# A new order for the first batch, the first scores of each batch and the last batch's weight splits in a packed-attention and SwiGLU kernel

## Chip, cores and metric

The kernel runs on one core of a Trainium2 chip. The metric is the device time of one execution in microseconds. "Before" is the median of three runs: 1436.34 us (1432.2 to 1437.11).

## What is computed

The reference has three parts, joined by one activation matrix x of 4608 tokens by 512:

```python
# attention: 8 batches, 8 heads, 576 positions, head size 64, 32 packing rows
p_packed = sm_attn(p, k, v)                 # "pack": softmax(p k^T / 8) v
out      = sm_attn(q, p_packed, p_packed)   # "unpack"
x = out.transpose(0, 2, 1, 3).reshape(4608, 512)
# SwiGLU
xn = x / sqrt(mean(x * x) + 1e-6) * rms_g
x  = (silu(xn @ w_gate) * (xn @ w_val)) @ w_out      # 512 -> 1536 -> 512
# bilinear
a, b = x @ w1, x @ w2
return ((a * b) @ w3) @ w_out2
```

The weights arrive as 64-bit floats. The kernel reads them as pairs of 32-bit words and builds 32-bit floats on the chip ("conversion").

## The kernel before

The program is one hand-written order. Python generators emit instructions, each engine runs its own instructions in the order of emission, and all loads and stores are issued by SyncE (SP), also in order. A wait at the head of an engine's queue holds all that stands behind it there.

**Conversion.** A `[128, 512]` block of 64-bit weights (0.52 MB) is loaded by `load64` (L99). `convert` then issues two ScalarE activations (`c_h` L108, `c_y` L109), two VectorE instructions (`c_t` L111, and the joining of sign and magnitude L112) and one GpSimd addition (L114). The gate and value weights `wgv` need 24 conversions, four for each of six column groups g.

**Attention of a batch.** `pack(b)` makes the packed rows: scores of p against k (PE L181), maximum (VectorE L185), exponential (ScalarE L188), transposes (PE L197) with copies (L198 on ScalarE, L199 on VectorE), the product with v (PE L208), scaling (L216), a transpose (L220) and the copies `bdP1T` (L224), `gP1T` (L226) and `bdG` (L239). `unpack(b)` takes q: scores against `bdP1T` (PE L262), transposes to `a2` on VectorE (L266), maximum, subtraction, exponential, sum and division, a transpose back to `a2T`, the norm of each token, and at the end the normalised activations split into a high part `ah` and a rest `al` (L55 on ScalarE, L56 on VectorE), as the matmuls need them.

**Dense units.** `wb_unit(b, g)` multiplies `gP1T` of batch b with column group g of `wgv` (PE L337) and splits the product into `wbh` and `wbl`. `dense_units(b)` then has 48 units, eight for each g; a unit is six matmuls into one PSUM bank (L376). Even units are evicted by a tanh on ScalarE (`th` L382) and VectorE (L383), odd ones by ScalarE (`vl` L387) and GpSimd (`ht` L388). Four banks ("gv") rotate through the units, two slots of two banks each ("at") through everything else. `wb_unit(b, g + 1)` stands after the fourth unit of group g.

**What sets the order.** `planned` runs `dense_units(b)` and, after the units whose numbers stand in a table, one step of another generator: `PACK` for `pack(b + 2)`, `UNPACK` for `unpack(b + 1)`, and two conversions of `w_out` per batch. In batch 0 the last 12 conversions of `wgv` take that place. Ahead of the first dense unit, the "front" is ordered by a string of letters: p (a step of pack 0 and then pack 1), u (unpack 0), c (a whole conversion, and the load of the block three further on), w (`wb_unit(0, 0)`), l (loads of later batches). In the last batch `first_loads` takes the place of the attention: its first step issues three loads of `w_out` rows, and each later step splits one row block into `wo_h` and `wo_l` (L55, L56), for the matmuls that follow the dense part. Its steps stand after the units 0, 3, 6, and so on up to 42.

After the dense part come the product with `w_out` (L566) and the bilinear stage (L811), which the change leaves alone.

Of the kernel before, what the change touches and what calls it, by code (L numbers as in the profile page):

```python
# [16 lines left out]
B, H, S, D = 8, 8, 576, 64  # L17
# [3 lines left out]
NC = H // 2  # L21
# [11 lines left out]
def packed_attention_swiglu_bilinear(ctx: ExitStack, tc, qT, kT, v, pT, rms_g, w_gv, w_out,  # L33
                                     w1, w2, w3T, w_out2, out):
    nc = tc.nc
# [49 lines left out]
    def load_k(b, parts=1):  # L85
        load("k", kT, b, 2, parts)

    def load_q(b):
        load("q", qT, b, 2)
# [7 lines left out]
    def load64(src):  # L97
        w = cv_of[0].tile([128, 512, 2], I32, tag="w64", name="w64", bufs=ahead64[0] + 1)
        nc.sync.dma_start(out=w.rearrange("p n t -> p (n t)"), in_=src.bitcast(I32))  # L99
        return w  # L100

    def convert(dst, w, shape):
        cv = cv_of[0]
        h = cv.tile([128, 512], F32, tag="c_h", name="c_h", bufs=2)
        y = cv.tile([128, 512], I32, tag="c_y", name="c_y", bufs=2)
        t = cv.tile([128, 512], I32, tag="c_t", name="c_t")
        d = dst.bitcast(I32)
        nc.scalar.activation(out=h, in_=w[:, :, 1].bitcast(F32), func=AF.Copy, scale=float(2.0 ** -112))  # L108
        nc.scalar.activation(out=y, in_=w[:, :, 0].bitcast(U32), func=AF.Copy, scale=float(2.0 ** -29))  # L109
        hi = h.bitcast(I32)  # L110
        nc.vector.tensor_scalar(out=t, in0=hi, scalar1=3, scalar2=None, op0=ALU.logical_shift_left)  # L111
        nc.vector.scalar_tensor_tensor(out=d, in0=shape(hi), scalar=-2 ** 31, in1=shape(t),  # L112
                                       op0=ALU.bitwise_and, op1=ALU.bitwise_or)
        nc.gpsimd.tensor_tensor(out=d, in0=d, in1=shape(y), op=ALU.add)  # L114

    def converting(jobs, take):


        n64 = ahead64[0]
        ahead = [load64(src) for src, *_ in jobs[:n64]]  # L120
        yield
        for i, job in enumerate(jobs):
            take(ahead.pop(0), *job[1:])
            if i + n64 < len(jobs):
                ahead.append(load64(jobs[i + n64][0]))
            yield
# [9 lines left out]
    converted = set()  # L136
    c_o_bufs = [2]

    def gv_weight(w, g, c):
        convert(wgv[:, c, :, 256 * g:256 * g + 256], w, lambda x: x.rearrange("p (a n) -> p a n", a=2))  # L140
        converted.add((g, c))

    def out_weight(w, dst):
        store_later(4, out=dst, in_=as_f32(w))
# [4 lines left out]
    pTs = att.tile([128, NC, B, NP], F32, name="pTs")  # L149
    nc.sync.dma_start(out=pTs, in_=pT)  # L150
    load_k(0, 2)
    gvw = converting([(w_gv[g, c], g, c) for g in range(6) for c in range(NC)], gv_weight)
# [92 lines left out]
    def unpack(b):  # L245
# [19 lines left out]
        for a, t in enumerate(ts):  # L265
            nc.vector.transpose(out=a2.rearrange("p e t n -> p e (t n)")[:, :, HALF * a:HALF * a + HALF],  # L266
                                in_=t[:, :, :HALF])
        yield
        if b:
            load_q(b + 2)  # L270
        for e in range(2):
            nc.vector.tensor_reduce(out=mx2[:, e], in_=a2[:, e], axis=AX.X, op=ALU.max)
            yield
            nc.vector.tensor_tensor(out=a2[:, e], in0=a2[:, e], in1=wide(mx2[:, e]), op=ALU.subtract)  # L274
            nc.scalar.activation(out=a2[:, e], in_=a2[:, e], func=AF.Exp, scale=SCALE)
            yield
# [52 lines left out]

    def wb_unit(b, g):  # L330
        gP1T = res["gP1T", b]
        while not all((g, c) in converted for c in range(NC)):
            next(gvw)
        t = slot("at")
        for c in range(NC):
            for e in range(2):
                nc.tensor.matmul(t[32 * c:32 * c + 32, e, :], lhsT=gP1T[64 * e:64 * e + 64, c, :],  # L337
                                 rhs=wgv[64 * e:64 * e + 64, c, :, 256 * g:256 * g + 256],
                                 start=True, stop=True, tile_position=(64 * e, 32 * c), skip_group_check=True)
        hi = dp.tile([128, 2, 512], F32R, tag="wbh", name="wbh", bufs=2)  # L340
        lo = dp.tile([128, 2, 512], F32R, tag="wbl", name="wbl", bufs=2)
        for e in range(2):
            split(hi[:, e], lo[:, e], t[:, e], nc.vector)
        wb[b, g] = (hi, lo)
# [58 lines left out]
    def drain(gen):  # L403
        for _ in gen:
            pass
# [16 lines left out]
    def chained(*gens):  # L422
        for g in gens:
            yield from g

    next(gvw)
    load_v(0)
    load_q(0)
    load_k(1)

    def planned(main, *others):

        for n, _ in enumerate(main):
            for at, gen in others:
                for _ in range(at.count(n)):
                    next(gen, None)
        for at, gen in others:
            for n in at:
                assert n < 60
            drain(gen)  # L440

    def wb_first():
        wb_unit(0, 0)
        yield

    def later():
        load_q(1)
        load_k(2)
        yield
        load_q(2)  # L450
        yield

    front = dict(p=chained(pack(0), pack(1)), u=unpack(0), c=gvw, w=wb_first(), l=later())
    for x in "pp c c p c pp c pp u c u u p u p u c w u u u c u uu p u c uu l pp c uu c uu pp c l c c":
        if x != " ":
            next(front[x])
    for x in "puw":
        drain(front[x])  # L460
    ow = converting([(w_out[128 * i:128 * i + 128, :], wo_d[128 * i:128 * i + 128, :]) for i in range(NF)], out_weight)

    PACK = [8, 8, 16, 31, 32, 40, 43]
    UNPACK = [0, 1, 3, 4, 6, 11, 13, 15, 17, 24, 24, 25, 31, 32, 40, 41, 42, 44]
    for b in range(B - 1):
        others = [(UNPACK, unpack(b + 1))]
        if b + 2 < B:
            others.insert(0, (PACK, pack(b + 2)))
        if b == 0:
            others.append(([1, 3, 5, 9, 12, 14, 18, 20, 22, 26, 28, 30], gvw))  # L470
        else:
            others.append(([21, 35], some(ow, 2)))
        planned(dense_units(b), *others)
# [42 lines left out]
    def first_loads():  # L516
        rows = [wo_d[128 * kk:128 * kk + 128, :] for kk in range(NF)]
        ahead = [fetch(x) for x in rows[:3]]
        yield
        for i in range(NF):  # L520
            split(wo_h[:, i], wo_l[:, i], ahead.pop(0), nc.gpsimd if i % 2 else nc.vector)
            if i + 3 < NF:
                ahead.append(fetch(rows[i + 3]))
            else:
                fetch_h(i + 3 - NF)
            yield
        fetch_h(3)
        for n in range(2):
            split_h(n)
            yield  # L530

    planned(dense_units(B - 1), (list(range(0, 45, 3)), first_loads()))
    flush()
    dp_ctx.close()
    wraw_ctx.close()
# [363 lines left out]
```

## Time and profile before

| | |
|---|---|
| median of the runs | 1436.34 us (1432.2 to 1437.11) |
| the profiled execution | 1431.36 us, span 1429.2 us |
| busy share of the span | PE 95%, VectorE (DVE) 55%, ScalarE (ACT) 38%, GpSimd (POOL) 34% |
| mean granted TensorE clock | 0.984 of full speed |
| chain that ended last, by engine | PE 80%, DVE 7%, ACT 3%, DMA 3%, issue 2% |
| first dense unit | 63.9 us after the span's start |
| last batch's dense units | from about 480.7 us |

The page of the profile gives busy time by engine. The timeline gives single instructions with start and duration, and in brackets the idle time of the engine just before one and what ended it. The view of waits sums such idle time by line and by what ended it, for a stretch. The view of windows gives the busy time of each engine in a stretch, with the granted clock.

### The profile page before, as it was taken

What the parts mean: (1) busy time and instruction counts of PE and PEld (TensorE: products, weight loads), DVE (VectorE), ACT (ScalarE), POOL (GpSimd) and SP (SyncE); (2) the same over time, 40 slices, a digit from 0 to 9 for tenths busy, and PEclk for the clock granted to TensorE, in tenths of its full rate; (3) what the DMA queues carried; (4) which work ended last, traced back from release to release, by engine and by line L of the source; (5) the groups of instructions that cost most, each with busy time, mean ns of one, the idle gap of its engine ahead of it and who ended that gap; (6) DMA issues with size and microseconds to landing.
All of it is one profiled execution on the core that took longest, in us unless ns stands there. A gap on an engine that the chain in (4) does not pass through costs nothing.

```text
span 1429.2 us, 22605 instructions
## 1 busy us (share of the span) xinstructions
PE 1353.3 (95%) x8824; PEld 1119.0 (78%) x8824; DVE 787.5 (55%) x1267; ACT 545.7 (38%) x1080; POOL 489.7 (34%) x438
## 2 busy tenths in 40 slices
PE   4579999999999899999999999999999999999988
PEld 2358878788788788888888877887888788788887
DVE  4787566766766547736177855335335343534443
ACT  3455455555555566525155542113112111211211
POOL 2456445445455452203034503322222222222111
PEclk9689999999999999999999999999999999999999
DMA  9853454443221357735369875434442643444263
GB/s 312 290 197 108 160 192 137 148 155 111 107 97 75 134 170 264 238 124 162 122 226 407 325 288 225 164 148 160 165 155 81 243 155 124 171 155 149 82 250 124
DMA packets 65562, 253.65 MB, mean 177 GB/s; under 512 B 7344, under 2 KB 7344, under 8 KB 55344
## 3 DMA queue, kind: packets, MB, share of 16 engines
q1 hardware_dynamic: 65456, 252.21, 49.8%
q8 instruction: 69, 1.13, 0.3%
q14 instruction: 37, 0.30, 0.1%
HBM read 185.08 MB, written 67.11 MB: 176 GB/s over the span
## 4 chain that ended last, share of the span: by engine, by line
PE 80%; DVE 7%; ACT 3%; DMA 3%; issue 2%; POOL 0%; SPq 0%; DVEq 0%; ACTq 0%; POOLq 0%
PE gv L811 24%; PE gv L376 17%; PE at L566 13%; PE gv L784 7%; PE at L784 7%; PE gv L566 5%; PE gv L658 3%; PE at L337 2%; DMA w<-ws_d 2%; DVE th L383 1%; PE at L292 1%; DVE a L274 1%; DVE wbl L56 1%; DVE wgv L112 1%; ACT vl L387 1%
## 5 line engine op out<-in xcount | busy, mean ns | idle before, releaser
L811 PE MATMUL gv<-xh,w 128*128 128x512 f32 (+1 forms) x1120 | 287.3, 371 | 10.1 <-DMA w<-ws_d 6.4
L55 ACT ACTIVATE hh<-hr 128x512 fp32r<-128x512 f32 (+1 forms) x148 | 91.0, 618 | 419.1 <-DVE hr L779 332.0
L811 PEld LDWEIGHTS gv<-xh,w 128*128 128x128 f32 x1120 | 201.1, 190 | 49.4 <-DMA w<-ws_d 7.6
L388 POOL TENSOR_TENSOR ht<-th,vl 128x288 f32<-128x288 f32 x192 | 163.7, 860 | 178.1 <-ACT vl L387 95.8
L376 PE MATMUL gv<-ah,wbh 128*128 128x288 f32 x768 | 178.7, 314 | 16.0 <-ACT vl L387 12.4
L376 PEld LDWEIGHTS gv<-ah,wbh 128*128 128x128 f32 x768 | 122.6, 190 | 67.6 <-issue 26.9
L838 POOL TENSOR_TENSOR u<-u,c 128x512 f32<-128x512 f32 (+1 forms) x40 | 63.9, 1598 | 319.9 <-DVE u L779 319.9
L376 PE MATMUL gv<-al,wbh 128*128 128x288 f32 x768 | 167.1, 298 | 0.0
L779 DVE TENSOR_TENSOR hr<-gv,hr 128x512 f32<-128x512 f32 (+1 forms) x80 | 51.0, 638 | 209.0 <-PE gv L811 209.0
L376 PE MATMUL gv<-ah,wbl 128*128 128x288 f32 x768 | 165.2, 296 | 0.0
L56 DVE TENSOR_TENSOR hl<-hr,hh 128x512 fp32r<-128x512 f32 (+1 forms) x148 | 130.2, 883 | 60.3 <-ACT hh L55 57.7
L811 PE MATMUL gv<-xl,w 128*128 128x512 f32 (+1 forms) x560 | 161.4, 370 | 0.0
L114 POOL TENSOR_TENSOR c_o<-c_o,c_y 128x512 int32<-128x512 int32 x52 | 73.9, 1421 | 206.6 <-DVE c_o L112 193.6
L376 PEld LDWEIGHTS gv<-al,wbh 128*128 128x128 f32 x768 | 125.2, 190 | 1.1 <-DVE al L56 0.9
L376 PEld LDWEIGHTS gv<-ah,wbl 128*128 128x128 f32 x768 | 124.4, 190 | 0.0
L383 DVE SCALAR_TENSOR_TENSOR th<-th,gv 128x288 f32<-128x288 f32 x192 | 84.3, 444 | 63.1 <-ACT th L382 62.2
L811 PEld LDWEIGHTS gv<-xl,w 128*128 128x128 f32 x560 | 102.1, 190 | 18.3
L566 PE MATMUL at<-hl,wo_h 128*128 128x512 f32 x288 | 112.3, 390 | 0.9 <-DVE hl L56 0.8
L566 PE MATMUL at<-hh,wo_h 128*128 128x512 f32 x288 | 112.2, 390 | 0.0
L566 PE MATMUL at<-hh,wo_l 128*128 128x512 f32 x288 | 112.1, 389 | 0.0
L387 ACT ACTIVATE vl<-gv 128x288 f32<-128x288 f32 x192 | 79.4, 414 | 58.6 <-PE gv L376 56.1
L56 DVE TENSOR_TENSOR wbl<-at,wbh 128x512 fp32r<-128x512 f32 x96 | 65.9, 686 | 60.4 <-ACT wbh L55 59.8
(125 smaller groups left out, 2341.9 us busy)
## 6 DMA issues: line engine op xcount, KB each, us to landing
w<-ws_d SPq DMA_DIRECT2D x40, 1792.0 KB, 7.5
hT_d<-ht SPq DMA_DIRECT2D x96, 288.0 KB, 2.7
hr<-hT_d SPq DMA_DIRECT2D x108, 256.0 KB, 4.7
ws_d<-stage SPq DMA_DIRECT2D x16, 896.0 KB, 8.6
w<-in_w_gv_dram SPq DMA_DIRECT2D x24, 512.0 KB, 7.0
w<-in_w_out_dram SPq DMA_DIRECT2D x20, 512.0 KB, 4.4
v<-in_v_dram SPq DMA_DIRECT2D x8, 1152.0 KB, 7.5
q<-in_qT_dram SPq DMA_DIRECT2D x8, 1152.0 KB, 7.1
```

Source lines behind the costliest of these rows:

```text
L55: nc.scalar.activation(out=hi, in_=src, func=AF.Copy)
L56: eng_lo.tensor_tensor(out=lo, in0=src, in1=hi.bitcast(F32), op=ALU.subtract)
L114: nc.gpsimd.tensor_tensor(out=d, in0=d, in1=shape(y), op=ALU.add)
L376: nc.tensor.matmul(t[:, :HALF], lhsT=w[:, e, 256 * i + 128 * f:256 * i + 128 * f + 128], rhs=x[:, e, HALF * hf:HALF * hf + HALF], start=(n ...
L383: nc.vector.scalar_tensor_tensor(out=th, in0=th, scalar=1.0, in1=t[:, :HALF], op0=ALU.add, op1=ALU.mult)
L387: nc.scalar.activation(out=vl, in_=t[:, :HALF], func=AF.Copy, scale=0.5)
L388: nc.gpsimd.tensor_tensor(out=ht[:, hf], in0=th, in1=vl, op=ALU.mult)
L566: nc.tensor.matmul(acc[m], lhsT=w[:, kk, 128 * m:128 * m + 128], rhs=x, start=(kk == 0 and a == 0), stop=(kk == NF - 1 and a == 2))
L779: nc.vector.tensor_tensor(out=out, in0=a, in1=b, op=op)
L784: nc.tensor.matmul(acc[m], lhsT=x[:, 128 * m:128 * m + 128], rhs=w[i], start=(i == 0 and n == 0), stop=(i == 7 and n == 2))
L811: nc.tensor.matmul(t, lhsT=wi[:, r, j, a], rhs=x[b][:, j, r, :w], start=(start and n == 0), stop=(n == 5), skip_group_check=True)
L838: nc.gpsimd.tensor_tensor(out=u2, in0=u2, in1=c22, op=ALU.mult)
```

## The change

Four things are changed.

1. A conversion is cut in two: `widened` (the two ScalarE instructions and the next load) and `joined` (VectorE and GpSimd). `gv_widen` and `gv_join` place them apart.
2. The front is written by the chain of batch 0. The letters are now a (widen), b (join), p (pack 0), q (pack 1, now a generator of its own), u, l, w. Eight of the 24 blocks are joined in the front, where ten were converted before the first dense unit and three more ahead of the first `th`; sixteen are joined inside batch 0, up to unit 32. A two-column exponential `warm` stands at the head of ScalarE's queue, ahead of the first widening. The load of q for batch 2 moves from the front to unit 20 of batch 0, and `unpack(b)` issues its load of q for b + 2 one step earlier.
3. `PACK` has its first two steps at 7 instead of 8, in the batches 0 to 5.
4. The last batch's `first_loads` has its first split at unit 9 instead of 3, and the later ones two or three units apart, up to 44.

```diff
-    def convert(dst, w, shape):
+    def widened(w):
...
         nc.scalar.activation(out=h, in_=w[:, :, 1].bitcast(F32), func=AF.Copy, scale=float(2.0 ** -112))
         nc.scalar.activation(out=y, in_=w[:, :, 0].bitcast(U32), func=AF.Copy, scale=float(2.0 ** -29))
+        return h, y
+
+    def joined(dst, hy, shape):
+        h, y = hy
+        t = cv_of[0].tile([128, 512], I32, tag="c_t", name="c_t")
...
+    def gv_widen():
+        i = len(gvhy)
+        if i < len(GV):
+            gvhy.append(widened(gv64[i]))
+            gv_load(1)
...
-        yield
         if b:
             load_q(b + 2)
+        yield
...
-    next(gvw)
+    gv_load(2)
     load_v(0)
     load_q(0)
+    gv_load(2)
     load_k(1)
+    warm = att.tile([128, 2], F32, name="warm")
+    nc.scalar.activation(out=warm, in_=ones, func=AF.Exp)
...
-    front = dict(p=chained(pack(0), pack(1)), u=unpack(0), c=gvw, w=wb_first(), l=later())
-    for x in "pp c c p c pp c pp u c u u p u p u c w u u u c u uu p u c uu l pp c uu c uu pp c l c c":
+    front = dict(p=pack(0), q=pack(1), u=unpack(0), l=later)
+    for x in "a pp b a p b pp pp u uu uu q q aa uu q b u b u uu a u w l b a u u q q b a uu uu q q b a b a l":
...
-    PACK = [8, 8, 16, 31, 32, 40, 43]
+    PACK = [7, 7, 16, 31, 32, 40, 43]
...
-            others.append(([1, 3, 5, 9, 12, 14, 18, 20, 22, 26, 28, 30], gvw))
+            others.append(([1, 3, 5, 8, 9, 12, 14, 16, 18, 20, 22, 25, 26, 28, 30, 32], joins()))
+            others.append(([20], later))
...
-    planned(dense_units(B - 1), (list(range(0, 45, 3)), first_loads()))
+    planned(dense_units(B - 1), ([0, 9, 11, 14, 17, 19, 22, 25, 28, 30, 33, 36, 38, 41, 44], first_loads()))
```

The line numbers in the rows of the changed kernel are those of its own file: L115 and L116 stand for L111 and L112, L210 and L211 for L185 and L186, L224 for L199, L241 for L216, L249 for L224, L251 for L226, L264 for L239, L291 for L266, L297 for L272, L299 for L274, L406 for L382, L407 for L383, L411 for L387.

**VectorE in the front**, from the reciprocal of batch 0's row sums to the first maximum of its unpack scores. Before:

```order
L201 RECIPROCAL rs<-rs 128x2
L111 TENSOR_SCALAR c_t<-c_h 128x512
L112 SCALAR_TENSOR_TENSOR wgv<-c_h,c_t 128x2x256
L216 TENSOR_SCALAR p_243<-at,rs 128x64 x2
L111 TENSOR_SCALAR c_t<-c_h 128x512
L112 SCALAR_TENSOR_TENSOR wgv<-c_h,c_t 128x2x256
L224 COPY bdP1T<-at 64x4x32 x2
L226 TENSOR_TENSOR gP1T<-at,gT 128x128
L239 COPY bdG<-at 32x2x32 x4
L266 STREAM_TRANSPOSE a_275<-at 128x2x288 x2
L111 TENSOR_SCALAR c_t<-c_h 128x512
L112 SCALAR_TENSOR_TENSOR wgv<-c_h,c_t 128x2x256
```

Of the change:

```order
L226 RECIPROCAL rs<-rs 128x2
L115 TENSOR_SCALAR c_t<-c_h 128x512
L116 SCALAR_TENSOR_TENSOR wgv<-c_h,c_t 128x2x256
L241 TENSOR_SCALAR p_237<-at,rs 128x64 x2
L249 COPY bdP1T<-at 64x4x32 x2
L251 TENSOR_TENSOR gP1T<-at,gT 128x128
L264 COPY bdG<-at 32x2x32 x4
L291 STREAM_TRANSPOSE a_259<-at 128x2x288 x2
L297 TENSOR_REDUCE mx_260<-a_259 128x18
```

The conversion between the scaling and `bdP1T` is gone, and so is the one behind the transposes. Further up, one conversion instead of two stands ahead of the copy of `a1T`.

**VectorE in batch 1**, around the first scores of batch 3 (`mx`, `nb`), with the unpack of batch 2 (`a`). Before:

```order
L383 SCALAR_TENSOR_TENSOR th<-th,gv 128x288
L274 TENSOR_TENSOR a_1494<-a_1494,mx_1495 128x576
L383 SCALAR_TENSOR_TENSOR th<-th,gv 128x288
L185 TENSOR_REDUCE mx<-at 128x1
L186 TENSOR_SCALAR nb<-mx 128x1
```

Of the change:

```order
L407 SCALAR_TENSOR_TENSOR th<-th,gv 128x288
L299 TENSOR_TENSOR a_1496<-a_1496,mx_1497 128x576
L210 TENSOR_REDUCE mx<-at 128x1
L211 TENSOR_SCALAR nb<-mx 128x1
L210 TENSOR_REDUCE mx<-at 128x1
L211 TENSOR_SCALAR nb<-mx 128x1
L407 SCALAR_TENSOR_TENSOR th<-th,gv 128x288 x2
```

The two maxima now stand directly behind the subtraction, ahead of the `th` of unit 8, which stood between.

**ScalarE at the start of the last batch** (`wbh` is the split of `wb_unit(7, 1)`). Before:

```order
L387 ACTIVATE vl<-gv 128x288
L55 ACTIVATE wo_h<-hr 128x512
L55 ACTIVATE wbh<-at 128x512 x2
L382 ACTIVATE th<-gv 128x288
L387 ACTIVATE vl<-gv 128x288
```

Of the change:

```order
L411 ACTIVATE vl<-gv 128x288
L55 ACTIVATE wbh<-at 128x512 x2
L406 ACTIVATE th<-gv 128x288
L411 ACTIVATE vl<-gv 128x288
L406 ACTIVATE th<-gv 128x288
L411 ACTIVATE vl<-gv 128x288
L406 ACTIVATE th<-gv 128x288
L411 ACTIVATE vl<-gv 128x288
L55 ACTIVATE wo_h<-hr 128x512
```

The first split of a `w_out` row block now stands three pairs of evictions later.

## Rows read from the trace of the kernel before

**Rows 1.** Page, busy tenths of TensorE in 40 slices of the span

```profile
PE   4579999999999899999999999999999999999988
```

**Rows 2.** Waits of TensorE, 137 to 196 us: total, times, longest us

```profile
PE at L337 <- ACT e L188: 1.4, 1, 1.4
```

**Rows 3.** Waits of TensorE, 196 to 254 us

```profile
PE at L337 <- ACT e L188: 1.0, 1, 1.0
```

**Rows 4.** Timeline, start of the last batch: start, duration, engine, line, instruction, [idle before]

```profile
480.74 0.54 PE L376 MATMUL gv<-ah,wbh 128*128 128x288 f32 x2
...
482.43 0.43 PE L376 MATMUL gv<-ah,wbh 128*128 128x288 f32 x2
...
485.49 0.63 ACT L55 ACTIVATE wo_h<-hr 128x512 fp32r<-128x512 f32 x1 [5.19 <-DMA hr<-wo_d]
...
488.73 0.85 PE L376 MATMUL gv<-ah,wbh 128*128 128x288 f32 x2 [4.55 <-ACT vl L387]
...
491.78 0.53 PE L376 MATMUL gv<-ah,wbh 128*128 128x288 f32 x2
```

**Rows 5.** Timeline, ScalarE's first exponential

```profile
10.53 1.28 ACT L188 ACT_TABLE_LOAD   x1 [10.53 <-DVE nb L186]
...
11.82 0.74 ACT L188 ACTIVATE e<-at,nb 128x576 f32<-128x576 f32 x1
```

**Rows 6.** Timeline, batch 0's chain in the front

```profile
12.79 2.77 PE L197 MATMUL at<-ident,e 128*96 128x128 f32 x12 [3.35 <-ACT e L188]
...
15.60 0.81 ACT L198 ACTIVATE a1T<-at 96x768 f32<-96x768 f32 x1
...
17.24 0.94 DVE L199 COPY a1T<-at 96x768 f32<-96x768 f32 x1
...
18.28 2.79 PE L208 MATMUL at<-v,a1T 96*32 96x64 f32 x96 [2.72 <-DVE a1T L199]
...
21.13 0.48 DVE L216 TENSOR_SCALAR p<-at,rs 128x64 f32<-128x64 f32 x2 [1.13 <-PE at L208]
...
21.66 0.48 PE L220 MATMUL at<-ident,p 128*128 128x128 f32 x1 [0.59 <-DVE p L216]
24.77 0.66 ACT L108 ACTIVATE c_h<-w 128x512 f32<-128x512 f32 x1 [7.25 <-DMA w<-in_w_gv_dram]
...
26.52 0.60 DVE L224 COPY bdP1T<-at 64x128 f32<-64x128 f32 x2
...
30.02 0.78 DVE L266 STREAM_TRANSPOSE a<-at 128x576 f32<-128x576 f32 x1 [0.38 <-PE at L262]
...
63.93 0.85 PE L376 MATMUL gv<-ah,wbh 128*128 128x288 f32 x2
```

**Rows 7.** Windows, 10 to 20 us: busy by engine, granted clock, DMA share, GB/s

```profile
10.00:20.00 10.00, 4.48 (x78) 4.02 (x82) 7.02 (x13) 6.98 (x12) 2.77 (x2) 1.00 1.03 318
```

**Rows 8.** Timeline, conversions at batch 0's first units

```profile
68.50 0.43 DVE L111 TENSOR_SCALAR c_t<-c_h 128x512 int32<-128x512 int32 x1
68.54 1.54 POOL L114 TENSOR_TENSOR wgv<-wgv,c_y 128x512 int32<-128x512 int32 x1 [0.70 <-DVE wgv L112]
...
68.96 1.67 DVE L112 SCALAR_TENSOR_TENSOR wgv<-c_h,c_t 128x512 int32<-128x512 int32 x1
...
73.63 0.69 DVE L112 SCALAR_TENSOR_TENSOR wgv<-c_h,c_t 128x512 int32<-128x512 int32 x1
```

**Rows 9.** Windows, 110 to 130 us

```profile
110.00:120.00 10.00, 10.00 (x170) 8.59 (x168) 9.08 (x14) 6.38 (x15) 8.61 (x9) 1.00 0.08 31
120.00:130.00 10.00, 10.00 (x87) 9.00 (x87) 4.42 (x12) 4.63 (x11) 7.12 (x9) 1.00 0.75 210
```

**Rows 10.** Timeline, a later batch around unit 8

```profile
318.00 0.69 DVE L56 TENSOR_TENSOR wbl<-at,wbh 128x512 fp32r<-128x512 f32 x1 [0.67 <-ACT wbh L55]
...
319.66 1.20 PE L181 MATMUL at<-k,pTs 64*32 64x288 f32 x32
...
324.46 1.09 PE L337 MATMUL at<-wgv,gP1T 64*32 64x512 f32 x16 [1.01 <-ACT e L188]
```

More of the change, by code (lines that the diff above doesn't have):

```diff
@@ L105, in convert @@
         y = cv.tile([128, 512], I32, tag="c_y", name="c_y", bufs=2)
-        t = cv.tile([128, 512], I32, tag="c_t", name="c_t")
-        d = dst.bitcast(I32)
         nc.scalar.activation(out=h, in_=w[:, :, 1].bitcast(F32), func=AF.Copy, scale=float(2.0 ** -112))
         nc.scalar.activation(out=y, in_=w[:, :, 0].bitcast(U32), func=AF.Copy, scale=float(2.0 ** -29))
+        return h, y
+    def joined(dst, hy, shape):
+        h, y = hy
+        t = cv_of[0].tile([128, 512], I32, tag="c_t", name="c_t")
+        d = dst.bitcast(I32)
         hi = h.bitcast(I32)
@@ L114, in convert @@
         nc.gpsimd.tensor_tensor(out=d, in0=d, in1=shape(y), op=ALU.add)
+    def convert(dst, w, shape):
+        joined(dst, widened(w), shape)
     def converting(jobs, take):
@@ L137, in packed_attention_swiglu_bilinear, with gv_load, gv_join @@
     c_o_bufs = [2]
-    def gv_weight(w, g, c):
-        convert(wgv[:, c, :, 256 * g:256 * g + 256], w, lambda x: x.rearrange("p (a n) -> p a n", a=2))
-        converted.add((g, c))
+    GV = [(g, c) for g in range(6) for c in range(NC)]
+    gv64, gvhy = [], []
+    def gv_load(n):
+        for _ in range(n):
+            i = len(gv64)
+            if i < len(GV):
+                gv64.append(load64(w_gv[GV[i]]))
+    def gv_widen():
+        i = len(gvhy)
+        if i < len(GV):
+            gvhy.append(widened(gv64[i]))
+            gv_load(1)
+    def gv_join():
+        i = len(converted)
+        if i < len(GV):
+            g, c = GV[i]
+            joined(wgv[:, c, :, 256 * g:256 * g + 256], gvhy[i], lambda x: x.rearrange("p (a n) -> p a n", a=2))
+            converted.add((g, c))
     def out_weight(w, dst):
@@ L151, in packed_attention_swiglu_bilinear @@
     load_k(0, 2)
-    gvw = converting([(w_gv[g, c], g, c) for g in range(6) for c in range(NC)], gv_weight)
     gT = att.tile([128, NC], F32, name="gT")
@@ L331, in wb_unit @@
         gP1T = res["gP1T", b]
-        while not all((g, c) in converted for c in range(NC)):
-            next(gvw)
+        assert all((g, c) in converted for c in range(NC))
         t = slot("at")
@@ L424, in chained @@
             yield from g
-    next(gvw)
+    gv_load(2)
     load_v(0)
     load_q(0)
+    gv_load(2)
     load_k(1)
+    warm = att.tile([128, 2], F32, name="warm")
+    nc.scalar.activation(out=warm, in_=ones, func=AF.Exp)
     def planned(main, *others):
@@ L440, in planned, with later_loads @@
             drain(gen)
-    def wb_first():
-        wb_unit(0, 0)
+    def later_loads():
+        load_q(1)
         yield
-    def later():
-        load_q(1)
         load_k(2)
@@ L451, in later, with joins @@
         yield
-    front = dict(p=chained(pack(0), pack(1)), u=unpack(0), c=gvw, w=wb_first(), l=later())
-    for x in "pp c c p c pp c pp u c u u p u p u c w u u u c u uu p u c uu l pp c uu c uu pp c l c c":
-        if x != " ":
+    later = later_loads()
+    front = dict(p=pack(0), q=pack(1), u=unpack(0), l=later)
+    for x in "a pp b a p b pp pp u uu uu q q aa uu q b u b u uu a u w l b a u u q q b a uu uu q q b a b a l":
+        if x in front:
             next(front[x])
-    for x in "puw":
-        drain(front[x])
+        elif x == "a":
+            gv_widen()
+        elif x == "b":
+            gv_join()
+        elif x == "w":
+            wb_unit(0, 0)
+    for x in "puq":
+        drain(front[x])
+    def joins():
+        for _ in GV:
+            gv_join()
+            gv_widen()
+            yield
     ow = converting([(w_out[128 * i:128 * i + 128, :], wo_d[128 * i:128 * i + 128, :]) for i in range(NF)], out_weight)
-    PACK = [8, 8, 16, 31, 32, 40, 43]
+    PACK = [7, 7, 16, 31, 32, 40, 43]
     UNPACK = [0, 1, 3, 4, 6, 11, 13, 15, 17, 24, 24, 25, 31, 32, 40, 41, 42, 44]
```

## Prediction

> **What bounds the kernel now.** I read the page first. Its slices of the span show TensorE (PE) busy in nine tenths or more nearly everywhere, and short of that in the first three slices, in the fourteenth (464 to 500 us) and in the last two [rows 1]: time is to be won where PE waits, most of all in the first 107 us (a slice is 35.7 us). The views of waits then say what ends PE's idle time in each batch. In the second batch the product with the weights (L337) waits 1.4 us for the exponential of the next packing, in the third 1.0 us [rows 2, 3]. The same line stands in the windows of the fourth to sixth batch with 1.0 us each; the seventh, which packs nothing, has none. Last I read the timeline at the three places that the change touches: the start of the last batch [rows 4], the front [rows 5, 6] and the first units of batch 0 [rows 8, 9].
>
> The sums are made against the profiled execution, 1431.36 us. The median of the runs is 5 us above it, so I take the middle of the two, 1433.9, as the time from which gains are subtracted. No change can be told from noise within 0.5% of the median, 7.2 us.
>
> **The last batch.** ScalarE's queue holds the split of the first weight block ahead of the evictions. It waits 5.19 us for the block's load, until 485.49, and PE, out of free banks, stands 4.55 us until 488.73 [rows 4]. The clock then falls to the lower of its levels: from 488.73 to 491.78 seven pairs start at half the pace. Six steps take 3.05 us where the six from 480.74 to 482.43 took 1.69, so 1.36 us more are lost. In the change the split stands behind unit 9. PE would be there at 480.74 plus nine units of 0.8 us (three pairs of 0.27), 488 or later, over 2 us after the block has landed. The loads are issued as early as before, so neither the wait nor the cold restart should remain: **5.9 us**. The later splits stand two or three units apart instead of three; ScalarE and VectorE have room for 12% more of them, which I cost at nothing. If that cover is thinner than I think, the lower end is 4.55 without the clock, or less.
>
> **The first scores at step 7.** Today the scores of the next-but-one batch follow unit 8 (L181, 1.20 us), and the product with the weights finds its slot still being read by the exponential: 1.01 us at 324.46 [rows 10]. One unit earlier gives 0.8 us, and the maxima also pass ahead of the `th` of unit 8 (0.4 us of VectorE's time and whatever it waited for). The exponential then ends some 1.2 us earlier, while PE comes to the product when it did, and the wait is gone. The scores bring a new wait: one of their two slots is freed by the split `wbl`, which ends at 318.69. Unit 8's scores started at 319.66; one unit earlier is 318.86, 0.17 us after it [rows 10]. And unit 8's `th` now waits for both exponentials on ScalarE, just before its bank is wanted again. I take the whole 1.4 + 4 x 1.0 = **5.4 us** for the batches 1 to 5, with 0 as the lower end.
>
> **The front.** Four steps of batch 0's chain are late for a reason that the change takes away.
> - ScalarE loads its function table only when the first exponential is due, 10.53 to 11.82 [rows 5]. The tiny exponential does it while the loads are under way: 1.3 us. By the Trainium skill (ScalarE: Activation LUTs, section "What ACT_TABLE_LOAD costs") a switch of the set costs 1.28 us and a drain of 1.38 on top, and moving it would save about 2.7. The row shows the exponential starting at the end of the load, with no drain behind it, so I keep 1.3.
> - The transposes (2.77 us) would end at 14.3 instead of 15.56 and ScalarE's copy (0.81) at 15.1. VectorE's copy, at 17.24 behind two conversions, has one ahead of it and is done by then. The product with v starts at 15.2 instead of 18.28: 3.1 us, the 1.3 included [rows 6].
> - Scaling at 21.13 and transpose at 21.66 take 0.48 each, so `bdP1T` could start at 22.2. It starts at 26.52, behind a conversion whose weights landed only at 24.77. That conversion is gone from this place. `bdP1T` starts at 19.1: 7.4 us in all, and the second score transpose, today over at 30.80, at 23.4.
> - From there to the first dense unit at 63.93, VectorE has six conversions in its queue before and four in the change, each 0.43 + 0.69 = 1.12 us [rows 6, 8]: 2.2 us. Against it stands batch 1's packing, whose maxima now precede the sums of batch 0. Its k has the same bytes ahead of it as the weight block that was read at 24.77; its scores take up to twice 1.20 us at the lower clock, so they are there at 27.2, while VectorE wants them at 26.4 (23.4 and four instructions of about 0.75). I charge 0.8 us.
>
> The loads of v and q for batch 0 move up by one weight block, 0.52 MB or 1.6 us at the 318 GB/s of this stretch [rows 7], and q, with 5.1 MB loaded by then, should be there at about 18, before it is wanted. The first dense unit would start at 63.9 - 7.4 - 2.2 + 0.8 = 55.1.
>
> **What is given back.** Ahead of the first `th` stand 13 conversions before and 8 in the change; of the three just before it, one goes (0.43 + 1.67 us [rows 8]). So the first `th` comes 8.8 + 2.1 = 10.9 us earlier, but five more conversions lie behind it. VectorE is 9.08 busy of 10 us from 110 to 120 and 4.42 in the next ten [rows 9]; until about 120 it has no room. I charge 5 x 1.12 = 5.6 us and keep **5.3 us** for front and batch 0 together. The ends are 10.9 (all five hidden in the later half of the batch) and 10.9 - 5 x 2.10 = 0.4 (each in the dear form).
>
> Sum: 5.9 + 5.4 + 5.3 = 16.6, so 1433.9 - 16.6 = **1417 us**. The move of the q loads I cost at nothing: no store stands between the old and the new place on SP's queue, and batch 2's q, now loaded at unit 20 of batch 0, is wanted after a further 28 units of 0.8 us.
>
> **Rivals.**
> - The conversions take the whole front gain back. An L112 started while GpSimd adds takes 1.67 us, against 0.69 alone [rows 8]. In the dense part GpSimd also multiplies every pair of units, so all five may be of that form: 0.4 + 5.4 + 5.9, 1422. The Trainium skill (SBUF — State Buffer, section "Who interferes with whom") states it as an exclusive lock between VectorE instructions with two SBUF inputs and GpSimd, by which the later one waits for the other's whole instruction; the 68.96 row, ending 0.55 us after GpSimd's, agrees. Against it: VectorE's slack after 120.
> - The scores at step 7 wait for `wbl`, or unit 8's `th` comes late, and PE loses there what it won: 5.3 + 5.9, 1423. The 0.17 us of margin speaks for it, the 1.2 us by which the slot is free sooner against it.
> - The give-back is hidden: 10.9 + 5.4 + 5.9, 1412.
> - Slower: the weight blocks starve ScalarE. Sixteen widenings lie inside batch 0 with `th` and `vl` behind them, and their loads share SP's queue with k, q and stores. One such wait took 7.25 us [rows 6]. If every one of the sixteen waits one transfer, 1.65 us, 26.4 are lost: 1433.9 - 16.6 + 26.4 = 1444. From 1.5 us each it is slower by over 0.5%. Four buffers, each loaded three blocks ahead, speak against it.
> - It does not do what it says: another load holds ScalarE in the last batch, and the first two rivals hold as well: 0.4 us, 1433.
>
> **How the numbers follow.** Forecast 0.44, conversions 0.20, step 7 0.14, give-back hidden 0.10, no effect 0.07, starved 0.05. Faster by over 0.5% takes in the first four, 0.88; the same 0.07; slower 0.05. The range leaves out the last two: from 1407 (the best case, and the runs' own spread of 5 us) to 1428 (the first two rivals together, 0.4 + 5.9, 1427.6).
>
> **What would show it.** In the changed profile: the table load near 1 us; `bdP1T` at about 19 and the first dense unit at about 55; no wait of L337 for the exponential in the windows of the later batches; the last batch without PE's 4.5 us for `vl`, and with the clock at its upper level. I am wrong if the first dense unit starts later than 60, if `th` of batch 0 waits for widenings that wait for loads, or if a new wait of over 0.5 us per batch stands before the scores at step 7.

## The result and the profile after

| | before | after |
|---|---|---|
| median | 1434.27 us (1431.2 to 1437.11, 4 runs) | 1419.63 us (1417.92 to 1421.43, 4 runs) |
| profiled execution, span | 1431.36, 1429.2 us | 1417.92, 1416.1 us |

The ratio is 0.990 with a 95% interval of 0.988 to 0.9921: 14.6 us are gained, where 16.6 were forecast, and the time lies in the range. Two of the twelve executions of p4_front, a kernel of the experiments below, and one of the kernel before measured beside it took 1701 us or more, far above the rest, and are left out of the ratios. The parts, however, did not come out as forecast. Three marks divide the span: the first dense unit, the unpack scores of batch 2 that open the next batch (L262, now L287), and those of batch 7. Between the marks, in the two profiled executions:

| stretch | before | after | gain |
|---|---|---|---|
| start to first dense unit | 63.93 | 52.95 | 11.0 |
| batch 0, first dense unit to the scores of batch 2 | 73.56 | 85.05 | -11.5 |
| batches 1 to 5, to the scores of batch 7 | 288.25 | 281.26 | 7.0 |
| the rest, with the last batch | 1003.46 | 996.84 | 6.6 |
| span | 1429.2 | 1416.1 | 13.1 |

The front won more than forecast, and batch 0 gave all of it back. The page shows where TensorE now falls short of nine tenths. Its busy tenths in 40 slices of the span:

```profile
PE   4788999999999999999999999999999999999988
```

The fourteenth slice, which was an 8 [rows 1], is a 9 now. The second and third are better (7 and 8 for 5 and 7), but the fourth, from 106 to 142 us, is an 8 where it was a 9: PE starts earlier and then waits.

**The front.** Timeline of the changed kernel, from the table load to the first `th`: start, duration, engine, line, instruction, [idle before <- what ended it]:

```profile
0.73 1.28 ACT L456 ACT_TABLE_LOAD   x1 [0.73 <-PEq L927]
...
10.56 0.74 ACT L213 ACTIVATE e<-at,nb 128x576 f32<-128x576 f32 x1 [0.57 <-DVE nb L211]
...
13.49 0.81 ACT L223 ACTIVATE a1T<-at 96x768 f32<-96x768 f32 x1
...
15.67 2.79 PE L233 MATMUL at<-v,a1T 96*32 96x64 f32 x96 [2.21 <-DMA v<-in_v_dram]
...
18.51 0.48 DVE L241 TENSOR_SCALAR p<-at,rs 128x64 f32<-128x64 f32 x2 [3.44 <-PE at L233]
...
19.69 0.61 DVE L249 COPY bdP1T<-at 64x128 f32<-64x128 f32 x2 [0.70 <-PE at L245]
...
24.61 2.17 PE L206 MATMUL at<-k,pTs 64*32 64x288 f32 x32 [1.50 <-DMA k<-in_kT_dram]
...
52.95 0.85 PE L400 MATMUL gv<-ah,wbh 128*128 128x288 f32 x2
...
57.90 0.45 DVE L407 SCALAR_TENSOR_TENSOR th<-th,gv 128x288 f32<-128x288 f32 x1 [0.49 <-ACT th L406]
```

The table load runs at 0.73, the first exponential at 10.56 instead of 11.82 [rows 5]. The copies of `a1T` are over at 14.30, and the product with v then waits for something new, the load of v, until 15.67. `bdP1T` starts at 19.69 instead of 26.52, and the first dense unit 11.0 us earlier [rows 6].

**Batch 0.** Timeline of TensorE, the products with the column groups of `wgv` (L361, which was L337), columns as above:

```profile
59.50 1.09 PE L361 MATMUL at<-wgv,gP1T 64*32 64x512 f32 x16
...
75.33 1.08 PE L361 MATMUL at<-wgv,gP1T 64*32 64x512 f32 x12
78.16 1.05 PE L361 MATMUL at<-wgv,gP1T 64*32 64x512 f32 x4 [1.75 <-POOL wgv L118]
...
88.82 2.23 PE L361 MATMUL at<-wgv,gP1T 64*32 64x512 f32 x12
93.37 1.05 PE L361 MATMUL at<-wgv,gP1T 64*32 64x512 f32 x4 [2.32 <-POOL wgv L118]
...
104.39 1.08 PE L361 MATMUL at<-wgv,gP1T 64*32 64x512 f32 x12
109.69 1.92 PE L361 MATMUL at<-wgv,gP1T 64*32 64x512 f32 x4 [4.22 <-POOL wgv L118]
...
122.38 1.08 PE L361 MATMUL at<-wgv,gP1T 64*32 64x512 f32 x12
123.92 1.05 PE L361 MATMUL at<-wgv,gP1T 64*32 64x512 f32 x4 [0.47 <-POOL wgv L118]
...
132.42 1.09 PE L361 MATMUL at<-wgv,gP1T 64*32 64x512 f32 x16
```

These six products make a ruler. Before, they started at 71.86, 88.92, 102.21, 113.12, 123.40 and 131.95. The changed kernel is ahead by 12.4, 13.6 and 13.4 us at the first three, by 8.7 at the fourth, 1.0 at the fifth, and 0.5 behind at the sixth. The lead is lost in two steps, 4.7 us after the third product and 7.7 after the fourth. In both the product has three quarters of its weights and waits for the last block, whose addition GpSimd has not made yet. The reasons differ. At the third product the block is late on VectorE, and the addition follows the joining at once, on a GpSimd that has stood idle for 1.35 us:

```profile
91.28 0.69 DVE L116 SCALAR_TENSOR_TENSOR wgv<-c_h,c_t 128x512 int32<-128x512 int32 x1
...
92.05 1.27 POOL L118 TENSOR_TENSOR wgv<-wgv,c_y 128x512 int32<-128x512 int32 x1 [1.35 <-DVE wgv L116]
```

So it is at the wait of 78.16 too. At the fourth product, the longest wait, it is GpSimd's queue, as its timeline with that of ScalarE, PE and VectorE shows:

```profile
105.80 1.26 POOL L412 TENSOR_TENSOR ht<-th,vl 128x288 f32<-128x288 f32 x1 [2.23 <-DVE c_t L115]
107.03 1.39 POOL L323 TENSOR_TENSOR sq<-sq 128x576 f32<-128x576 f32 x1
108.38 2.48 POOL L118 TENSOR_TENSOR wgv<-wgv,c_y 128x512 int32<-128x512 int32 x2
109.67 0.67 ACT L107 ACTIVATE c_y<-w 128x512 int32<-128x512 uint32 x1 [4.30 <-POOL wgv L118]
...
109.69 1.92 PE L361 MATMUL at<-wgv,gP1T 64*32 64x512 f32 x4 [4.22 <-POOL wgv L118]
...
111.53 0.85 PE L400 MATMUL gv<-ah,wbh 128*128 128x288 f32 x2
111.65 0.60 ACT L55 ACTIVATE wbh<-at 128x512 fp32r<-128x512 f32 x1 [1.02 <-PE at L361]
...
112.28 0.69 DVE L56 TENSOR_TENSOR wbl<-at,wbh 128x512 fp32r<-128x512 f32 x1 [5.86 <-ACT wbh L55]
```

VectorE has joined the block by 104.58, but its addition stands in GpSimd's queue behind a unit's `ht`, which itself started after 2.23 us of idle time, and behind the squares. PE stands 4.22 us. ScalarE stands 4.30 us as well: its next widening wants one of the two `c_y` buffers, which that addition still reads. VectorE then has no `wbh` to split for 5.86 us. The dense pairs from 112.18 to 115.06 start 0.48 us apart, where 0.27 is usual, as at the lower level of the clock; the stretch from 107.95 to 112.95 has a granted clock of 0.53. Before, the stretch between the fourth and fifth product had no wait at all.

The whole batch, as the groups of the products show it, before and in the change (count | busy us, mean ns | idle before):

```profile
L337 PE MATMUL at<-wgv,gP1T 64*32 64x512 f32 x96 | 6.5, 600 | 2.2 <-ACT e L188 1.2 <-DVE a L266 1.0
```

```profile
L361 PE MATMUL at<-wgv,gP1T 64*32 64x512 f32 x96 | 12.6, 620 | 8.9 <-POOL wgv L118 8.8
```

The products cost 12.8 us more, and only half of that is shown as waiting: a product that is cut in two takes 1.08 us for its first twelve matmuls and 1.05 for the last four, where all sixteen take 1.09. The 2.23 us at 88.82 hold one more such cut, since the third block's addition ended at 89.95, and the 1.92 us at 109.69 fall in the stretch with the clock of 0.53. Against this the dense pairs wait 6.6 us less for evictions than before (1.3 for 7.9), and take 3.1 us longer; the scores of batch 2 wait 3.5 us, for k and for `wbl`.

**Batches 1 to 5 and the last one.** Waits of TensorE, 306 to 364 us: total, times, longest us.

```profile
PE gv L400 <- ACT vl L411: 0.3, 1, 0.3
```

The wait for the exponential [rows 2, 3] is gone from all five batches: 1.4 + 4 x 1.0. The wait for `vl`, 0.6 in each before, is 0.5, 0.8, 0.3, 0.3 and 0.3 now, 0.8 less in sum. The last batch is seen in the window from 470 to 490 us: busy time by engine (PE, PEld, DVE, ACT, POOL), granted clock, DMA share, GB/s.

```profile
470.00:490.00 20.00, 20.00 (x172) 16.84 (x171) 11.64 (x21) 14.06 (x33) 13.46 (x15) 1.00 0.57 193
```

PE is busy throughout, the clock at its upper level; the 4.55 us for `vl` and the slow pairs behind them [rows 4] are gone.

### The profile page after: what moved, and what is told of

It is laid out like the page before. It is cut to its first block, busy times and chain, and to the rows that moved or that the text cites. A ratio compares the mean times of both kernels' runs of the same rounds, so it can differ in the third digit from the quotient of the medians.

```text
span 1416.1 us, 22596 instructions
## 1 busy us (share of the span) xinstructions
PE 1360.6 (96%) x8824; PEld 1121.8 (79%) x8824; DVE 787.3 (56%) x1267; ACT 546.4 (39%) x1081; POOL 488.7 (35%) x438
## 4 chain that ended last, share of the span: by engine, by line
PE 78%; DVE 5%; DMA 5%; ACT 3%; issue 2%; POOL 1%; SPq 0%; DVEq 0%; ACTq 0%; POOLq 0%
PE gv L850 23%; PE gv L400 17%; PE at L605 11%; PE gv L823 7%; PE at L823 7%; PE gv L605 5%; PE gv L697 3%; DMA w<-ws_d 3%; PE at L361 3%; DMA hr<-hT_d 1%; PE at L317 1%; DVE th L407 1%; ACT th L406 1%; DVE stage L56 1%; DMA ws_d<-stage 1%
## 5 line engine op out<-in xcount | busy, mean ns | idle before, releaser
L407 DVE SCALAR_TENSOR_TENSOR th<-th,gv 128x288 f32<-128x288 f32 x192 | 84.4, 445 | 55.8 <-ACT th L406 53.4
L411 ACT ACTIVATE vl<-gv 128x288 f32<-128x288 f32 x192 | 79.3, 413 | 58.4 <-PE gv L400 56.7
```

The costliest lines, as they stand in the source:

```text
L407: nc.vector.scalar_tensor_tensor(out=th, in0=th, scalar=1.0, in1=t[:, :HALF], op0=ALU.add, op1=ALU.mult)
L411: nc.scalar.activation(out=vl, in_=t[:, :HALF], func=AF.Copy, scale=0.5)
```

## The experiments

Twelve kernels were run. This table has their stretches as above (profiled executions, us); the time is the median where there is an interval, otherwise a single run.

| kernel | time | first dense unit | batch 0 | batches 1 to 5 | rest |
|---|---|---|---|---|---|
| before | 1434.27 | 63.93 | 73.56 | 288.25 | 1003.46 |
| after | 1419.63 | 52.95 | 85.05 | 281.26 | 996.84 |
| p1_pack7 | 1427.35 | 64.46 | 73.86 | 281.59 | 1005.29 |
| p2_splits9 | 1428.39 | 64.76 | 75.18 | 288.11 | 998.55 |
| p3_pack7_splits9 | 1418.03 | 65.02 | 72.32 | 281.21 | 996.15 |
| p4_front | 1433.49 | 52.76 | 86.02 | 288.55 | 1004.77 |
| m1_widen3 | 1416.70 | 52.94 | 84.67 | 280.27 | 997.02 |
| m3_joins | 1416.97 | 52.99 | 83.74 | 281.17 | 997.30 |
| m6_loads | 1416.92 | 53.81 | 83.51 | 280.97 | 996.81 |
| x1_noadd | 1404.05 | 53.18 | 73.01 | 280.74 | 995.37 |
| n1_joins_widen3 | 1413.03 | 53.84 | 79.39 | 280.54 | 997.53 |
| n2_joins_widen3_loads | 1411.82 | 53.03 | 80.94 | 280.84 | 995.59 |
| n3_add_dve | 1414.04 | 52.82 | 81.83 | 280.69 | 996.56 |
| f1_ten_in_front | 1413.55 | 55.59 | 79.02 | 280.90 | 995.79 |

How far one profile can be trusted, the table shows itself. The kernel before and p2 have the same front and batch 0, and so have p1 and p3, yet batch 0 differs by 1.6 and by 1.5 us; the rest, among kernels with the same splits, differs by up to 3.2. A difference of 1.5 us between two rows is therefore nothing.

### The parts alone

Four kernels are the one before with one or two parts of the change. The edit of `PACK` alone (p1), of the last batch's splits alone (p2), both (p3), and the new front alone (p4, whose diff is the front's part of the change above):

```diff
-    PACK = [8, 8, 16, 31, 32, 40, 43]
+    PACK = [7, 7, 16, 31, 32, 40, 43]
```

```diff
-    planned(dense_units(B - 1), (list(range(0, 45, 3)), first_loads()))
+    planned(dense_units(B - 1), ([0, 9, 11, 14, 17, 19, 22, 25, 28, 30, 33, 36, 38, 41, 44], first_loads()))
```

> The kernel before with the first scores at step 7 and the last batch's splits from unit 9, and the old front. Theory A (the new front wins about 11 us up to the first dense unit and batch 0 gives all of it back): this takes the whole gain, 13 to 14 us off the kernel before, 1420 to 1421, as fast as the whole change or a little faster. Theory B (the front keeps its 5.3 us, as predicted, and the other two parts are worth less): some 9 us off, 1425.

> The change with the scores back at step 8 and the splits back at units 0, 3, 6 and on: the new front alone. Theory A: first dense unit near 53 us, the second scores of batch 2 near 137.5 to 138 as in the kernel before, time within 2 us of before. Theory B: 5 us faster than before. Rival C (batch 0 gives its gain back only because step 7 makes its scores of batch 2 wait for the load of k and for the slot): batch 0 is 3.5 us shorter than in the whole change and the time 3 to 4 us below before.

> The kernel before with the first scores at step 7 alone. From the first scores of batch 2 to those of batch 7 the kernel before takes 288.2 us; if the five waits of L337 for the exponential are all, 282.8 (5.4 less); if the wait for the evictions behind them shortens too, as in the whole change, 281.3 (7.0 less). Batch 0 as before, or up to 1 us shorter.

> The kernel before with the last batch's splits from unit 9 alone. The idle stretch of 4.5 us at the start of the last batch is gone and the clock stays at its upper level; profiled time 5.9 us below the kernel before's (6.6 us by what the whole change shows after its last batch begins). Nothing else moves.

With both edits and the old front the median was 1418.03 us, ratio 0.9889 (0.9873 to 0.9905); with the front alone 1433.49, ratio 1.0002 (0.9989 to 1.0015). So the whole gain is made without the front, and the front by itself is worth nothing that can be measured. p1 and p2 put the two gains where they were expected, 6.7 us in the batches 1 to 5 and 4.9 in the rest; what else moved in them, up to 1.8 us, is hardly more than two profiles of the same stretch differ by. p4 also has the waits of batch 0, 9.2 us for the addition, and its batch 0 is no shorter than that of the whole change: the loss belongs to the front and not to the scores at step 7, and rival C falls.

### The waits of batch 0, one at a time

The joins placed earlier (m3), a third buffer for `c_y` with one taken from `c_o` (m1), and batch 2's k loaded earlier (m6), each on top of the change:

```diff
-            others.append(([1, 3, 5, 8, 9, 12, 14, 16, 18, 20, 22, 25, 26, 28, 30, 32], joins()))
+            others.append(([1, 3, 4, 6, 7, 9, 11, 13, 15, 17, 19, 21, 23, 25, 27, 29], joins()))
```

```diff
-        y = cv.tile([128, 512], I32, tag="c_y", name="c_y", bufs=2)
+        y = cv.tile([128, 512], I32, tag="c_y", name="c_y", bufs=c_y_bufs[0])
...
-    c_o_bufs = [2]
+    c_o_bufs = [1]
+    c_y_bufs = [3]
```

```diff
-    for x in "a pp b a p b pp pp u uu uu q q aa uu q b u b u uu a u w l b a u u q q b a uu uu q q b a b a l":
+    for x in "a pp b a p b pp pp u uu uu q q aa uu q b u b u uu a u w l l b a u u q q b a uu uu q q b a b a":
...
-            others.append(([20], later))
+            others.append(([36], later))
```

> The whole change with the sixteen joins in batch 0 two to three units further ahead of the products that need them (steps 1, 3, 4, 6, 7, 9, 11, 13, 15, 17, 19, 21, 23, 25, 27, 29). The length of batch 0, from the first dense unit to the first scores of batch 2, is 85.0 us in the whole change and 73.6 before. Theory J (the products L361 wait for additions of blocks that are joined only two or three units before: 8.8 us in four waits): the waits nearly vanish and the length falls to 76 to 79. Theory V (VectorE is the bound, 45 of 52 us busy until 105 us): the waits only change their name, length 83 to 86.

> The whole change with three instead of two buffers for the low words (c_y), and one instead of two for the converted w_out block. Theory W (the widening stands a block ahead, fills both buffers and waits on ScalarE for GpSimd's addition, 8.5 us in eight waits, with the evictions of the dense units behind it): those waits go and batch 0 falls to 79 to 81. Theory J or V: the waits go and the length stays within 2 us of 85.

> The whole change with k of batch 2 loaded directly behind q of batch 1 in the front, and q of batch 2 at unit 36 instead of 20. Theory L (batch 0 loses time to loads that come late or collide: 1.5 us for k at the scores, and GpSimd's product at 105.8 us, idle for 2.2 us, waiting for a store queued behind q): the scores no longer wait for k, GpSimd's pause goes, length of batch 0 80 to 82. Theory J or V: within 2 us of 85.

Each shortened batch 0 by little, 1.3, 0.4 and 1.5 us, no more than two profiles of the same batch differ by. The waits of TensorE in batch 0 (total, times, longest us) show that the time was renamed. Of m3:

```profile
PE gv L400 <- ACT vl L411: 8.3, 3, 4.0
```

Of m1:

```profile
PE at L362 <- POOL wgv L118: 10.2, 5, 4.3
```

With the joins earlier, no product waits for an addition any more, but ScalarE still waits 7.7 us in seven places for `c_y`, its `vl` stand behind that, and PE waits 8.3 us for them. With a third `c_y`, ScalarE's waits for it are gone and PE's for the addition grow from 8.8 to 10.2. In m6 the load of k is no longer waited for, but the scores then wait 3.9 us for `wbl`, and the additions are waited for 10.3 us in place of 8.8. Each single fix leaves another of the waits to end last (theory V in the text on m3).

### What the addition itself costs

```diff
-        nc.gpsimd.tensor_tensor(out=d, in0=d, in1=shape(y), op=ALU.add)
+        if not 8 <= len(converted) < 24:
+            nc.gpsimd.tensor_tensor(out=d, in0=d, in1=shape(y), op=ALU.add)
```

> The whole change with GpSimd's addition left out for the sixteen blocks joined inside batch 0 (their weights then lack the low word's share). This takes away GpSimd's leg of the conversion, its share of the port that it has with VectorE, and the widening's wait. Theories J and W: length of batch 0 74 to 77. Theory V with VectorE's own instructions alone: 82 or more. Theory V with the dear form (L116 and L115 lengthened beside additions): below 77, with fewer instructions of L116 over 1.1 us.

Batch 0 fell to 73.01 us, 12.0 less, and the time to 1404.05. This is the length that it had with the old front, though four more conversions lie in it: 18 from the first dense unit on, 14 before. The comparison is not a clean one, since the kernel before paid for its own fourteen additions in that length, and no run took those away. It shows what sixteen additions cost in the changed kernel, and not that they are all of the loss. The length lies just under the 74 to 77 of theories J and W, and also fits theory V with the dear form: three instructions of L116 take over 1.1 us here, six in the change. How the additions reached the other engines is seen on VectorE, first in its waits in batch 0 of the changed kernel, then of x1:

```profile
DVE wbl L56 <- ACT wbh L55: 13.6, 10, 5.9
```

```profile
DVE wbl L56 <- ACT wbh L55: 7.0, 10, 1.4
```

and in its groups of instructions from 52.95 to 138.00 us of the changed kernel, then from 53.18 to 126.19 of x1 (count | busy us, mean ns | idle before):

```profile
L116 DVE SCALAR_TENSOR_TENSOR wgv<-c_h,c_t 128x512 int32<-128x512 int32 x18 | 16.2, 898 | 0.6
...
L299 DVE TENSOR_TENSOR a<-a,mx 128x576 f32<-128x576 f32 x2 | 3.4, 1692 | 0.0
```

```profile
L116 DVE SCALAR_TENSOR_TENSOR wgv<-c_h,c_t 128x512 int32<-128x512 int32 x18 | 14.4, 800 | 0.6
...
L300 DVE TENSOR_TENSOR a<-a,mx 128x576 f32<-128x576 f32 x2 | 1.5, 751 | 0.0
```

VectorE's busy time in the batch fell from 63.51 to 59.62 us, 3.9, in instructions that had run beside GpSimd's additions; its idle time fell by 8.1 (21.5 to 13.4), 6.6 of it before `wbl`. So of VectorE's time the longer instructions, on which the prediction's first rival rested, are the smaller part here, and waiting is the larger. The Trainium skill (SBUF — State Buffer, section "Who interferes with whom") has a VectorE instruction with two SBUF inputs contend with a GpSimd instruction that reads SBUF, for a pair of ports that one holds at a time; the subtraction, which has two and took 1.69 us in the change and 0.75 in x1, agrees. On VectorE that comes to no more than 3.9 of the 12.0 us.

### Two waits at once

Since the two waits for GpSimd stood in for one another, n1 has the edits of m3 and m1 together, and n2 that of m6 as well. n3 instead gives every second addition to VectorE:

```diff
-        nc.gpsimd.tensor_tensor(out=d, in0=d, in1=shape(y), op=ALU.add)
+        eng = nc.vector if 8 <= len(converted) < 24 and len(converted) % 2 else nc.gpsimd
+        eng.tensor_tensor(out=d, in0=d, in1=shape(y), op=ALU.add)
```

> The earlier joins and the third c_y buffer together (with one buffer for the converted w_out block). Theory G (GpSimd's addition holds batch 0 in two ways that stand in for each other: the product L361 waits for it, and the widening on ScalarE waits for it with the evictions behind; each fix alone moves the wait to the other): both waits shrink, the length of batch 0 from the first dense unit falls from 85 to 75 to 79, the time 6 to 10 us below the change. Theory V (VectorE is full, and the fixes only rename its waits): length 82 or more, time within 2 us of the change.

> The same with k of batch 2 loaded earlier and q of batch 2 later. Theory G: 1 to 3 us below the kernel without the moved loads, since k no longer holds the scores at step 7. Theory V: within 2 us of the change.

> The whole change with every second addition of the sixteen blocks in batch 0 on VectorE instead of GpSimd, the fourth block of each group among them. VectorE gains eight instructions of some 0.7 us, 5.6 us; GpSimd loses eight of 1.27 us. Theory G: the additions that the products wait for follow the joining at once, the waits of L361 for GpSimd go, and batch 0 falls to 75 to 80 although VectorE does more. Theory V: it grows by up to 5.6 us, to 86 to 90.

n1 took 5.7 us from batch 0, where its two edits alone took 1.3 and 0.4 (theory G in the time, 6.6 us below the change; its batch is 0.4 us over the 75 to 79 that it gave). Its median is 1413.03 (1412.69 to 1415.4), ratio 0.9861 (0.9844 to 0.9879), an interval that ends where that of the change begins (0.988). n2 has 1411.82 (1411.4 to 1412.8), ratio 0.9849 (0.9835 to 0.9864). It is the best version measured of those that do the whole work, and beats the kernel before and the change; n1 and n2 can't be told apart, and n2's batch 0 is not shorter, so the earlier load of k is not shown to help. n3, a single run, took 3.2 us from batch 0, which is between what the two theories gave it, so that neither is borne out: PE's waits for the addition became 10.6 us of waiting for VectorE's.

What holds n1 in batch 0 is now ScalarE again, with `vl` waited for three times, 8.8 us. The timeline of n1 at the longest, VectorE, ScalarE and PE:

```profile
82.07 0.79 DVE L115 TENSOR_SCALAR c_t<-c_h 128x512 int32<-128x512 int32 x1
...
82.89 1.53 DVE L116 SCALAR_TENSOR_TENSOR wgv<-c_h,c_t 128x512 int32<-128x512 int32 x1
84.34 0.68 DVE L56 TENSOR_TENSOR wbl<-at,wbh 128x512 fp32r<-128x512 f32 x1
...
85.06 0.60 ACT L55 ACTIVATE wbh<-at 128x512 fp32r<-128x512 f32 x1 [2.81 <-DVE wbl L56]
...
86.31 0.53 PE L401 MATMUL gv<-ah,wbh 128*128 128x288 f32 x2 [4.07 <-ACT vl L412]
```

A conversion stands ahead of `wbl` on VectorE; the second `wbh` waits 2.81 us for that `wbl`, the `vl` stands behind it, and PE waits 4.07. That conversion takes 0.79 and 1.53 us, the dear form. In the whole batch n1 has eleven such L116 of over 1.1 us, the change six, and VectorE is busy 68.1 us, 4.6 more than in the change and 8.5 more than in x1, while the batch is 6.4 us longer than in x1. So the first rival's cause, small in the change, grows when the waits go. A second thing is left in n1: ScalarE stands 7.7 us ahead of four `c_h`, for which the profile names no releaser; each of them starts 0.09 us after the end of an L116, which frees one of the two `c_h` buffers. That this is the reason is inferred; no run gave `c_h` a third buffer.

The last kernel tried to take a conversion away from there: n1 with ten blocks joined in the front and fourteen in batch 0.

```diff
-    for x in "a pp b a p b pp pp u uu uu q q aa uu q b u b u uu a u w l b a u u q q b a uu uu q q b a b a l":
+    for x in "a pp b a p b pp pp u uu uu q q aa uu q b u b u uu aa u b w l b a u u q q b a b a uu uu q q b a b a l":
...
-            others.append(([1, 3, 4, 6, 7, 9, 11, 13, 15, 17, 19, 21, 23, 25, 27, 29], joins()))
+            others.append(([4, 6, 8, 10, 11, 13, 15, 17, 19, 21, 23, 25, 27, 29], joins()))
```

> The kernel with earlier joins and three c_y buffers, with ten instead of eight blocks joined in the front: one more ahead of the split of the first product, one more behind the scaling of batch 1's packed rows, where VectorE waits for TensorE and GpSimd. VectorE is busy 31 of the 44 us between the first maximum and the first dense unit. Theory P (a conversion is nearly free where VectorE waits and costs some 3 us behind the first dense unit, as 85.0 against 73.6 us for four more of them in batch 0): the first dense unit comes at 54 to 55.5 instead of 53.8, batch 0 takes 73 to 76 instead of 79.4, the time is 3 to 5 us below that kernel's 1413.0. Theory Q (a conversion costs its 1.1 us of VectorE wherever it stands): the first dense unit 2 us later, batch 0 2 us shorter, the time within 1.5 us of 1413.

The first dense unit came 1.75 us later and batch 0 was 0.4 us shorter; 1413.55 (1411.26 to 1415.41), ratio 0.9856 (0.9837 to 0.9876), cannot be told from n1. The time is as theory Q had it, and theory P falls; but of the 2 us that theory Q took from batch 0 hardly anything came. The same wait stands at the same place, longer:

```profile
86.13 0.85 PE L401 MATMUL gv<-ah,wbh 128*128 128x288 f32 x2 [5.26 <-ACT vl L412]
```

So conversions are not simply traded between front and batch 0. What would remove this wait stays open: no run moved the conversion away from between `wbh` and `wbl` alone.

## Why the prediction was right, and where it was wrong

The time was right, with the sum of its parts partly right by chance.

**The last batch: right in its mechanism, a little too small.** 5.9 us were forecast, and both the wait and the slow clock are gone. The rest of the program is shorter by 6.6 us in the two profiles: PE waits 4.5 us less for `vl`, is busy 1.3 less, and waits 0.7 less for the weights of the bilinear stage (5.7 for 6.4), which the edit does not touch. Over the eleven profiled kernels with the new splits it has 996.7 us in the mean, over the three without (before, p1, p4) 1004.5. That is 7.8, of which the term explains 5.9; where the remainder comes from is not shown.

**The first scores at step 7: right, a little too small.** The wait of 5.4 us went entirely. The stretch gained 7.0, the means over all kernels 7.4. PE's idle time in it (stretch less busy time) fell from 8.73 to 2.43 us, 6.3, which is the 5.4 and 0.8 less waiting for `vl`; 0.7 is in busy time. The rival, that the scores wait for `wbl` or k, is true of batch 0 alone: 1.99 us for `wbl` and 1.48 for k there, nothing in the later batches.

**The front: right, a little too small.** The table load was worth 1.26 us for 1.3 forecast. The Trainium skill (ScalarE: Activation LUTs, section "What ACT_TABLE_LOAD costs") would have had 2.7; the run agrees with the row and not with it. `bdP1T` starts at 19.69 for 19.1 forecast, because the product waits for the load of v, which the forecast had not counted. From there to the first dense unit it takes 33.3 us, where 36.0 were forecast and 37.4 measured before: batch 1's maxima, charged with 0.8, made VectorE wait for nothing, and the rest of this gain is not explained. The first dense unit starts at 52.95 for 55.1, the first `th` 12.8 us earlier for 10.9.

**What is given back: the step that failed.** The prediction charged "5 x 1.12 = 5.6 us" for the conversions that now lie inside batch 0, with an end of 5 x 2.10 if each were in the dear form. The batch became 11.5 us longer, and front and batch 0 together gained -0.5 where 5.3 were forecast, at or just under the lower end of 0.4. The place was right. The price was not, because it counted only the time that VectorE works on a conversion. That part came true: from the first dense unit on, batch 0 has four conversions more, 4.5 us at the charged price, and VectorE is busy 63.5 us for 58.3 before, 5.2 more. But it is also idle 6.3 us more (21.5 for 15.3), and this term the sum put at nothing. A conversion passes through three engines, and the next product waits for the last of them: TensorE waited 8.8 us for the additions, where before it waited for none, and its products took 6.1 us longer besides.

The first rival named the loss and gave a cause that fits it badly: had these four come in the dear form of 2.10, VectorE would be busy 8.4 us more, not 5.2. How the loss divides is shown in part only. With the waits for GpSimd removed, n1 wins back 5.7 us; the rest of the 11.5 stays open, with VectorE's dear form and the buffers of `c_h` as its candidates. The profile before had a sign: GpSimd, 34% busy over the span, is 60% busy in batch 0 (43.9 of 73.6 us), and the rows from which the prediction read VectorE's room have GpSimd at 8.61 and 7.12 of 10 us [rows 9]. That column I had not weighed. Nor did any sign of being wrong look at the length of batch 0: none of them came, while the term was lost.

**The other rivals.** That widenings starve for loads fell: ScalarE has no wait for a weight load in batch 0 of the changed kernel; its one wait without a named releaser, 2.84 us ahead of a `c_h` at 55.28, ends 0.09 us after an L116. That the change does nothing, and that the give-back is hidden, fell with the rest.

The errors cancel, which is luck: the two edits of the tables, forecast 11.3, are worth some 15 us together (p3: 1418.03 against 1433.33), and the front, forecast 5.3, nothing.

## What to carry to other kernels

Work that is pushed out of a serial start into a dense phase can cost more there than the busy time of the engine that it loads most: here 11.5 us for 5.6, since products waited for the end of a chain through three engines. Ask of each link what stands ahead of it in its engine's order, and who waits for the last. If removing a wait changes the time by less than the wait, look for a second one that now ends last, and remove the two together before giving the idea up: alone they gave 1.3 and 0.4 us here, which one profile cannot tell from nothing, together 5.7. And run each part of a change by itself: a total that agrees with a sum does not say that its terms do.

## What was not expected of the hardware

In n3 the addition of 32-bit integers, which takes GpSimd 1.29 us in the mean in batch 0 of the changed kernel (23.2 us for 18), shows on VectorE as a custom operation on 16-bit halves of 934 ns. Group of instructions of n3 in batch 0, columns as above:

```profile
L119 DVE CUSTOM_DVE_ANT_0 wgv<-wgv,c_y 128x1024 uint16<-128x1024 uint16 x8 | 7.5, 934 | 0.4
```

It is cheaper than on GpSimd, and dearer than the 0.42 to 0.69 us of the two conversion instructions that VectorE has already.
